# Output projection in blocks of 126 features, the last group of heads taken straight from SBUF, and half of the second projection's blocks summed earlier

## Chip, cores and metric

One core of a Trainium2 chip runs the whole program. The metric is the device time of one execution in microseconds. The core has a matrix engine (PE, its weight loads shown as PEld), a vector engine (DVE), an activation engine (ACT), a general engine (POOL), and SyncE (SP), which here only issues DMAs. Each engine takes its instructions in the order in which the program lists them and waits for the others through semaphores.

## The reference

Two independent parts are computed and set side by side in the output's columns (2048 rows, 576 + 576 columns):

```python
# A: sliding-window attention, 32 heads of 18 features, window 256, over x (2048 x 576)
q, k, v = x @ wqkv                       # per head
p = softmax(where(0 <= i - j < 256, q k^T / sqrt(18), -1e9))
a = concat_heads(p @ v) @ wo             # wo: 576 x 576
# B: a state-space convolution over u (2048 x 576)
K = real(sum_n C[d,n] dB[d,n] exp(dt A[d,n] l))
b = causal_conv(u, K) + u * Dskip
out = concatenate([a, b], axis=-1)
```

## The kernel before

A first part (up to about 550 us) projects q, k and v, builds the convolution's taps, and writes the intermediate results to DRAM. The second part, `attention`, is one hand-written instruction order for all engines: no scheduler moves anything.

**Units and items.** Attention works in 16 units: 2 halves of 1024 queries by 8 groups of 4 heads (unit i has half i // 8, group i % 8). A unit has 6 items (2 chunks of 512 queries by 3 banks of score blocks), so there are 96 items; the loop runs n from 0 to 97. In step n, `merge` interleaves several generators by their share of work done: the scores and exponentials of item n (`scores`, PE then ACT, then POOL's triangular masks), row maxima of a later unit (`gmax`, PE then DVE), the weighted values of item n - 2 (`values`, PE), 2 or 3 steps of the convolution (`conv`), and, from n = 64, one step of the output projection of the first half in every second n (`wo(0)`).

**Convolution.** `conv` has 16 rounds of transforms on PE, ACT, DVE and POOL, then 16 rounds that read its result back (tiles ho and tx from h), load u on POOL's queue (tiles X and t), multiply it by Dskip on POOL, and add on DVE. The second kind of round runs in about the last 20 steps.

**Quotients.** `values` accumulates 4 heads in one PSUM tile of 128 rows: each head has 32 rows, 18 of values, and its row 18 is the softmax denominator. After a chunk's last bank ACT copies it to `osb` (line 704). After a unit's last item `norm` is appended to a list and advanced one yield per step n: four small DMAs bring the denominators into 128x32 (`den`, line 714); a reciprocal (line 717); a spread to 128x1024 (line 720); a matmul with a block matrix `same` copies it to all rows of a head (line 726); DVE multiplies (727); ACT makes the fp16 high part (728) and DVE the low part (730); POOL's queue stores 18 rows of each head to the DRAM tensor `od`, high and low parts (734). After the loop the list is run to its end.

**Output projection.** `od` has 576 features by 2048 positions, twice. `wo_load` splits wo into `woh` and `wol` with 5 blocks of rows: four of 128 features and a last one in which 64 features stand twice, for the high and the low part. `wo_operands(c)` loads 512 positions of `od` in four DMAs on SP (lines 846 to 849). `wo(hf)` has 16 steps for two chunks c, each for 128 positions by 288 output columns: 14 matmuls (5 high x high, 5 high x low, 4 low x high; line 173), a scaled copy by ACT from PSUM (line 862), and after two steps a DMA of 128 output rows (`ya`, two buffers; `after(1, ...)` issues it one item later). `wo(0)` is spread over the items; `wo(1)` runs alone after everything else.

All small PSUM results (gmax, conv, norm, wo) take turns in one pool `ring` of three banks, so a matmul group waits until the group three before it has been evacuated.

## Time and profile before

| | us |
|---|---|
| runs shown: median (lowest, highest) | 1151.99 (1150.27, 1154.17) |
| the profiled execution, its own time | 1151.56 |
| its span, first to last instruction | 1149.8 |
| PE busy | 912.0 (79%) |
| DVE busy | 704.7 (61%) |
| ACT busy | 624.3 (54%) |
| POOL busy | 527.1 (46%) |

All times of rows are microseconds from the span's start unless marked ns. A row of the timeline gives start, duration, engine, line, operation, tiles (out<-in), shape and count; in square brackets stands how long the engine was idle before it and what ended that. A row of the chain gives start, duration, engine and line. A row of the busy time by stretch gives, for each engine, the busy time and the number of instructions, then the granted PE clock (1.00 is full), the mean busy share of the 16 DMA engines and GB/s. A row of the groups gives line, engine, operation, count, busy time and mean ns, then idle time before the group. Matmuls are pipelined, so the busy time of one is longer than its share of a stream of them.

### The profile page before, as it was taken

How to read it: one execution, taken by the hardware profiler on the slowest of the kernel's cores; microseconds unless marked ns; L12 is line 12 of the kernel's file. 1: busy time of each engine (PE TensorE's matmuls, PEld its weight loads, DVE VectorE, ACT ScalarE, POOL GpSimd, SP SyncE). 2: the span in 40 equal slices, each digit the busy share in tenths (PEclk: the TensorE clock that was granted, in tenths of full speed). 3: DMA queues.
4: the chain of work that ended last, by engine and by line, in shares of the span. 5: the costliest groups of instructions: out<-in, count | busy, mean ns of one | idle time of the engine just before them, and what ended most of it. 6: DMA issues, size and time to landing. Idle time of an engine off the chain costs nothing.

```text
span 1149.8 us, 26992 instructions
## 1 busy us (share of the span) xinstructions
PE 912.0 (79%) x10380; PEld 446.9 (39%) x10380; DVE 704.7 (61%) x1789; ACT 624.3 (54%) x955; POOL 527.1 (46%) x626
## 2 busy tenths in 40 slices
PE   1535979897978889866888889888889899896648
PEld 0313546455545655423333333333333333332216
DVE  2879656866776552366666778777776665653220
ACT  1785778767878742331455555555655554544312
POOL 0014324543545330102356656667666655679810
PEclk9757889898989889997799999999999999988859
DMA  9564423433342325984334554644336453558742
GB/s 271 150 190 137 101 46 89 109 92 86 84 109 59 78 61 128 228 247 131 98 120 125 140 151 138 169 132 136 110 107 166 134 160 110 166 153 227 202 123 84
DMA packets 157682, 153.59 MB, mean 134 GB/s; under 512 B 37777, under 2 KB 136017, under 8 KB 157361
## 3 DMA queue, kind: packets, MB, share of 16 engines
q1 hardware_dynamic: 149600, 132.68, 42.6%
q0 software_dynamic: 6448, 15.19, 5.0%
q10 hardware_dynamic: 1504, 3.99, 1.3%
q8 instruction: 82, 1.34, 0.5%
q14 instruction: 48, 0.39, 0.1%
HBM read 89.79 MB, written 61.60 MB: 132 GB/s over the span
## 4 chain that ended last, share of the span: by engine, by line
PE 46%; DVE 17%; DMA 13%; ACT 9%; issue 7%; POOL 6%; SPq 2%; DVEq 0%; ACTq 0%; POOLq 0%
PE pp L173 8%; PE po L696 6%; PE r L637 5%; PE r L501 5%; PE r L173 4%; PE r L508 3%; PE r L726 3%; PE ST L673 3%; PE kp L419 3%; PE pp L462 3%; DMA K<-in_wqkv_dram 2%; PE x L315 2%; DMA gk<-g 2%; POOL P L684 2%; DVE qb L629 1%
## 5 line engine op out<-in xcount | busy, mean ns | idle before, releaser
L640 DVE CUSTOM_DVE_ANT_0 jk<-r,bias 128x288 f32<-128x288 f32 (+7 forms) x512 | 206.6, 435 | 113.4 <-PE r L637 110.7
L675 ACT ACTIVATE P<-ST,esc 128x1024 f32<-128x1024 f32 (+1 forms) x192 | 203.3, 1060 | 95.5 <-PE ST L673 89.7
L381 POOL TENSOR_TENSOR m<-A,tr 128x1024 f32<-128x1024 f32 x72 | 149.3, 2094 | 195.4 <-PE kp L419 139.0
L684 POOL TENSOR_SCALAR_AFFINE_SELECT P<-P 128x512 f32<-128x512 f32 x240 | 158.2, 690 | 99.5 <-ACT P L675 97.3
L637 PE MATMUL r<-K,qb 128*64 128x288 f16 (+7 forms) x1024 | 134.3, 300 | 27.0 <-DVE t L528 6.2
L696 PE MATMUL po<-P,V 128*32 128x256 f32 (+2 forms) x1408 | 116.9, 404 | 4.7 <-ACT osb L704 2.2
L536 POOL TENSOR_TENSOR Y<-t,t 64x288 f32<-64x288 f32 x64 | 54.5, 852 | 140.0 <-DVE t L531 86.6
L637 PEld LDWEIGHTS <-qb 128*64 128x64 f16 x1024 | 60.3, 111 | 129.7 <-issue 75.9
L419 PE MATMUL kp<-Q,m 128*32 128x64 f32 x4608 | 87.4, 228 | 26.4 <-DVE Q L402 10.8
L419 PEld LDWEIGHTS kp<-Q,m 128*32 128x32 f32 x4608 | 74.4, 115 | 55.0 <-issue 42.9
L462 PE MATMUL pp<-ut,w 128*128 128x288 f32 x128 | 51.9, 530 | 43.3 <-DMA ut<-in_u_dram 22.9
L673 PE MATMUL ST<-Q,K 64*128 64x384 f16 (+2 forms) x704 | 75.3, 284 | 2.4 <-DMA Q<-m 2.4
L728 ACT ACTIVATE oh<-osb 128x512 f16<-128x512 f32 x32 | 20.2, 630 | 103.8 <-DVE osb L727 103.8
L238 DVE SCALAR_TENSOR_TENSOR qst<-pp,qst 128x512 f16<-128x512 f32 x36 | 24.7, 686 | 65.3 <-ACT qst L237 65.2
L726 PE MATMUL r<-spread,heads 128*128 128x512 f32 x64 | 40.1, 715 | 27.1 <-DVE spread L720 18.9
L129 ACT ACTIVATE g<-pp 128x288 f32<-128x288 f32 (+1 forms) x84 | 34.3, 447 | 39.7 <-DMA gk<-g 21.1
L501 PE MATMUL r<-tx,w 128*64 128x288 f32 x256 | 46.9, 447 | 11.0 <-DMA tx<-gx 9.5
L537 POOL TENSOR_TENSOR Y<-t,t 64x288 f32<-64x288 f32 x64 | 53.4, 835 | 3.8
L462 PEld LDWEIGHTS pp<-ut,w 128*128 128x128 f32 x128 | 28.6, 242 | 63.5 <-issue 19.0
L327 ACT ACTIVATE ab<-k 128x512 f32<-128x512 f32 (+1 forms) x54 | 31.9, 590 | 38.3 <-DVE k L326 37.9
L508 PE MATMUL r<-Y,i 128*128 128x288 f32 x128 | 49.1, 466 | 3.5 <-DVE m L640 1.5
L173 PE MATMUL pp<-xh,wl 128*128 128x512 f16 x180 | 49.0, 396 | 0.0
(159 smaller groups left out, 1743.7 us busy)
## 6 DMA issues: line engine op xcount, KB each, us to landing
gx<-g SPq DMA_DIRECT2D x32, 288.0 KB
qd<-qst SPq DMA_DIRECT2D x72, 128.0 KB
gk<-g SPq DMA_DIRECT2D x16, 576.0 KB
tx<-gx SPq DMA_DIRECT2D x16, 576.0 KB
tk<-gk SPq DMA_DIRECT2D x16, 576.0 KB
h<-ho SPq DMA_DIRECT2D x16, 576.0 KB
raw<-in_xT_dram SPq DMA_DIRECT2D x16, 512.0 KB
Q<-qd SPq DMA_DIRECT2D x32, 216.0 KB
```

The source lines that it names most:

```text
L173: self.nc.tensor.matmul(ps, u, v, start=(i == 0), stop=(i == len(ops) - 1))
L381: self.nc.gpsimd.tensor_tensor(m, A[:, ch, a0:a0 + 8].unsqueeze(3).to_broadcast(sh), tr[:, ch, part, 0:8].unsqueeze(2).to_broadcast(sh), o ...
L419: nc.tensor.matmul(kp[32 * st:32 * st + 32, c % 2 * JJ2 + j, :], m[:, ch, a0:a0 + 32], Q[:, ch, term % 2, :], start=(term == 0), stop=(ter ...
L462: nc.tensor.matmul(ps, self.w1[:, part, :], src[:, o:o + k], start=True, stop=True)
L501: nc.tensor.matmul(ps[64 * par:64 * par + 64], w2[:, par, 64 * part:64 * part + 64], t[:, 2 * hs:2 * hs + 2, par, :], start=True, stop=True)
L508: nc.tensor.matmul(ps, i1[:, par, :], Y[par], start=True, stop=True)
L637: nc.tensor.matmul(ps[64 * b:64 * b + 64, :n], self.qb[:, b, t, :], d["K"][:, b, k0:k0 + n], start=True, stop=True, skip_group_check=True)
L640: nc.vector.tensor_tensor_reduce(out=jk[:, :n], in0=ps[:, :n], in1=self.bias[:, 288 - n:], scale=1.0, scalar=-3e38, op0=OP.add, op1=OP.max ...
L673: nc.tensor.matmul(ps[:, u, o:o + n], d["K"][h, jp, k0:k0 + 128], d["Q"][h, jp, q0:q0 + n], start=True, stop=True, skip_group_check=True)
L675: nc.scalar.activation(pt[:, 2 * jp:2 * jp + 2, lo:hi], ps[:, :, lo:hi], AF.Exp, scale=self.esc)
L684: nc.gpsimd.affine_select(v, v, pattern=[[0, 4], [sg, 128]], compare_op=OP.is_ge, fill=0.0, base=-1 if far else 0, channel_multiplier=-sg)
L696: nc.tensor.matmul(self.po[32 * j:32 * j + 32, t0 * 128:t1 * 128], V[:, kb * 76 + 19 * j:kb * 76 + 19 * j + 32], pt[:, j, o:o + (t1 - t0) ...
```

## The change

- wo's rows are laid out on the host as four blocks of 126 features (7 heads of 18) and a fifth block with the last group of 4 heads (72 features) at rows 0 to 17 of each 32, the layout that a normalised unit has in SBUF. `wo_load` loads each column slice with one DMA.
- Units 7 and 15, the last group of each half, are no longer stored to `od`: their quotients stay in a tile `h7` and feed the fifth block directly. A step of the projection has 12 matmuls on four blocks and 3 on `h7`.
- Unit 15 gets its own normalisation, `norm_last`, for each chunk of 512: a matmul with a new block matrix `sums` puts each head's denominator on all its rows, DVE takes the reciprocal of 128x512, multiplies, and the two parts go to `h7`. The first chunk is begun at n = 95, the second after the loop.
- The first half's projection (`wo_first`) runs spread over n = 62 to 85.
- For the second half, blocks 0 and 1 are loaded at n = 84 and 88 and summed in n = 87 to 96 (`wo_part`, 16 steps of 6 matmuls); ACT copies the scaled sums to tiles that the convolution no longer uses. After the loop `wo_operands` loads blocks 2 and 3, and `wo_rest` has 16 steps of 9 matmuls; DVE adds the stored sum at evacuation.

The diff:

```diff
@@ -72,12 +72,15 @@
         bias[p, 1, p % 32 + 1:] = -1e30
     c["c_w1"], c["c_w2"], c["c_i1"], c["c_i2"] = w1, w2, i1, i2
     c["c_id"], c["c_bias"] = np.eye(128), bias
-    c["c_heads"] = np.concatenate([np.kron(np.eye(4), np.ones((32, 32))), np.tile(np.eye(32), (4, 1))], axis=1)
+    row = np.zeros((32, 32))
+    row[18] = 1.0
+    c["c_heads"] = np.concatenate([np.kron(np.eye(4), np.ones((32, 32))), np.tile(np.eye(32), (4, 1)),
+                                   np.kron(np.eye(4), row)], axis=1)
     return {k: np.ascontiguousarray(v.astype(ml_dtypes.bfloat16 if k in mult else np.float32)) for k, v in c.items()}
 
 
 def merge(*streams):
-    live = [[g, n, 0] for g, n in streams]
+    live = [[g, n, 0] for g, n in streams if n]
     while live:
         s = min(live, key=lambda t: t[2] / t[1])
         try:
@@ -598,9 +601,9 @@
                 nc.vector.memset(d["K"][h + 32:h + 64], -32768.0)
             self.sets.append(d)
         self.od = self.p["dram"].tile([2, D, L], F16, name="od")
-        hd = ap.tile([128, 160], F32, name="heads")
+        hd = ap.tile([128, 288], F32, name="heads")
         nc.sync.dma_start(hd, a["c_heads"])
-        self.same, self.pick = hd[:, 0:128], hd[:, 128:160]
+        self.same, self.pick, self.sums = hd[:, 0:128], hd[:, 128:160], hd[:, 160:288]
 
     def cols(self, hf):
         q0 = HQ * hf
@@ -703,6 +706,21 @@
                 self.osb[i] = self.p["o"].tile([128, HQ], F32, name="osb")
             nc.scalar.activation(self.osb[i][:, c * 512:c * 512 + 512], self.po, AF.Copy)
 
+    def norm_last(self, c):
+
+        nc, osb, cs = self.nc, self.osb[15], slice(c * 512, c * 512 + 512)
+        ps = self.p["ring"].tile([128, 512], F32, name="r")
+        nc.tensor.matmul(ps, self.sums, osb[:, cs], start=True, stop=True)
+        rb = self.p["n1"].tile([128, 512], F32, name="rb")
+        nc.vector.reciprocal(rb, ps)
+        yield
+        h = self.h7[1]
+        nc.vector.tensor_tensor(osb[:, cs], osb[:, cs], rb, op=OP.mult)
+        nc.scalar.activation(h[:, 0, cs], osb[:, cs], AF.Copy)
+        yield
+        nc.vector.tensor_tensor(h[:, 1, cs], osb[:, cs], h[:, 0, cs], op=OP.subtract)
+        yield
+
     def norm(self, i):
 
 
@@ -719,7 +737,10 @@
         sh = [128, 32, 32]
         nc.vector.tensor_tensor(X, den.unsqueeze(1).to_broadcast(sh), self.pick.unsqueeze(2).to_broadcast(sh), op=OP.mult)
         yield
-        h = np_.tile([128, 2, HQ], F16, name="oh16")
+        if i == 7:
+            h = self.h7[0] = self.p["h7"].tile([128, 2, HQ], F16, name="h7")
+        else:
+            h = np_.tile([128, 2, HQ], F16, name="oh16")
         for c in range(2):
             cs = slice(c * 512, c * 512 + 512)
             ps = self.p["ring"].tile([128, 512], F32, name="r")
@@ -729,7 +750,7 @@
             yield
             nc.vector.tensor_tensor(h[:, 1, cs], osb[:, cs], h[:, 0, cs], op=OP.subtract)
         yield
-        for j in range(4):
+        for j in range(4 if i != 7 else 0):
             f0 = 72 * g + 18 * j
             nc.gpsimd.dma_start(self.od[:, f0:f0 + 18, HQ * hf:HQ * hf + HQ].rearrange("a p n -> p a n"),
                                 h[32 * j:32 * j + 18])
@@ -743,7 +764,7 @@
         merge((self.gmax(0), 35), (part(conv, 12), 12))
         self.begin(1)
         items = [(i, c, b) for i in range(16) for c in range(2) for b in range(3)]
-        wo0, wl = self.wo(0), self.wo_load()
+        wo0, wo1, wl, self.acc, self.h7 = self.wo_first(), self.wo_part(), self.wo_load(), [], {}
         for n in range(len(items) + 2):
             self.begin(n)
             streams = []
@@ -776,28 +797,41 @@
                 streams.append((part(conv, k), k))
             if 20 <= n < 52 and n % 2 == 0:
                 next(wl, 0)
-            if n in (60, 72):
-                self.wo_operands((n - 60) // 12)
-            if n >= 64 and n % 2 == 0:
-                streams.append((part(wo0, 1), 1))
+            if n in (59, 67):
+                self.wo_operands((n - 59) // 8, 0, 4)
+            if 62 <= n < 86:
+                k = share(n - 62, 16, 24)
+                streams.append((part(wo0, k), k))
+            if n == 86:
+                for _ in wo0:
+                    pass
+            if n in (84, 88):
+                self.wo_operands(2 + (n - 84) // 4, 0, 2)
+            if 87 <= n < 97:
+                k = share(n - 87, 16, 10)
+                streams.append((part(wo1, k), k))
+            if n == 95:
+                self.h7[1] = self.p["h7"].tile([128, 2, HQ], F16, name="h7")
+                norms.append(self.norm_last(0))
             merge(*streams)
             norms = [g for g in norms if next(g, 0) is None]
-            if n >= 2 and (n - 2) % 6 == 5:
+            if n >= 2 and (n - 2) % 6 == 5 and n < 97:
                 norms.append(self.norm(items[n - 2][0]))
                 next(norms[-1])
-        for g in norms:
-            for _ in g:
-                pass
+        norms.append(self.norm_last(1))
+        while norms:
+            norms = [g for g in norms if next(g, 0) is None]
         for n in range(3):
             self.begin(len(items) + 2 + n)
             for _ in conv:
                 pass
-        for _ in wo0:
+        for _ in wo1:
             pass
-        self.wo_operands(2)
-        self.wo_operands(3)
-        for _ in self.wo(1):
-            pass
+        for c in (2, 3):
+            self.wo_operands(c, 2, 4)
+        for c in (2, 3):
+            for _ in self.wo_rest(c):
+                pass
 
     def wo_load(self):
         nc, a, wp = self.nc, self.a, self.p["wo"]
@@ -808,7 +842,7 @@
 
         def raw(c):
             t = wp.tile([128, 5, 144], F32, name="raw%d" % (c % 2))
-            self.load_rows(t, a["wo"], slice(c % 4 * 144, c % 4 * 144 + 144))
+            nc.sync.dma_start(t, a["wo"][:, :, c % 4 * 144:c % 4 * 144 + 144])
             return t
 
         nx = raw(0)
@@ -838,34 +872,63 @@
                 nc.vector.scalar_tensor_tensor(self.osc, self.pz, 2.0 ** -13, po, op0=OP.mult, op1=OP.mult)
                 yield
 
-    def wo_operands(self, c):
-
-        nc, wp, cs = self.nc, self.p["wo2"], slice(c * 512, c * 512 + 512)
-        oh = wp.tile([128, 5, 512], F16, name="oh")
-        ol = wp.tile([128, 4, 512], F16, name="ol")
-        nc.sync.dma_start(oh[:, 0:4], self.od[0, 0:512, cs].rearrange("(k p) n -> p k n", p=128))
-        nc.sync.dma_start(oh[0:64, 4], self.od[0, 512:576, cs])
-        nc.sync.dma_start(oh[64:128, 4], self.od[1, 512:576, cs])
-        nc.sync.dma_start(ol, self.od[1, 0:512, cs].rearrange("(k p) n -> p k n", p=128))
-        self.ops[c] = oh, ol
-
-    def wo(self, hf):
-        nc, a, wp = self.nc, self.a, self.p["wo2"]
-        for c in range(2 * hf, 2 * hf + 2):
-            oh, ol = self.ops[c]
+    def wo_operands(self, c, k0, k1):
+
+        nc, cs = self.nc, slice(c * 512, c * 512 + 512)
+        if c not in self.ops:
+            self.ops[c] = [self.p["wo2"].tile([126, 4, 512], F16, name=n) for n in ("oh", "ol")]
+        for e, t in enumerate(self.ops[c]):
+            nc.sync.dma_start(t[:, k0:k1], self.od[e, 126 * k0:126 * k1, cs].rearrange("(k p) n -> p k n", p=126))
+
+    def wo_mm(self, c, t, h, k0, k1, last):
+
+        ps = self.p["ring"].tile([128, 512], F32, name="r")[:, :288]
+        (oh, ol), ts, ws = self.ops[c], slice(t * 128, t * 128 + 128), slice(h * 288, h * 288 + 288)
+        ops = [(o[:, k, ts], w[0:126, k, ws]) for k in range(k0, k1)
+               for o, w in ((oh, self.woh), (oh, self.wol), (ol, self.woh))]
+        if last:
+            x, o = self.h7[c // 2], c % 2 * 512 + t * 128
+            ops += [(x[:, e, o:o + 128], w[:, 4, ws]) for e, w in ((0, self.woh), (0, self.wol), (1, self.woh))]
+        for i, (l, r) in enumerate(ops):
+            self.nc.tensor.matmul(ps, l, r, start=(i == 0), stop=(i == len(ops) - 1))
+        return ps
+
+    def wo_first(self):
+
+        for c in range(2):
             for t in range(4):
-                y = wp.tile([128, D], F32, name="ya")
+                y = self.p["wo2"].tile([128, D], F32, name="ya")
                 for h in range(2):
-                    ps = self.p["ring"].tile([128, 512], F32, name="r")
-                    self.mm14(ps[:, :288], (self.woh, self.wol), (oh, ol), slice(h * 288, h * 288 + 288),
-                              slice(t * 128, t * 128 + 128), flip=True)
-                    nc.scalar.activation(y[:, h * 288:h * 288 + 288], ps[:, :288], AF.Copy, scale=self.osc)
+                    ps = self.wo_mm(c, t, h, 0, 4, True)
+                    self.nc.scalar.activation(y[:, h * 288:h * 288 + 288], ps, AF.Copy, scale=self.osc)
                     yield
                 r = c * 512 + t * 128
-                if hf:
-                    nc.sync.dma_start(a["out"][r:r + 128, 0:D], y)
-                else:
-                    self.after(1, nc.sync.dma_start, a["out"][r:r + 128, 0:D], y)
+                self.after(1, self.nc.sync.dma_start, self.a["out"][r:r + 128, 0:D], y)
+
+    def wo_part(self):
+
+        p, acc = self.p, self.acc
+        for i in range(2):
+            t = p["fs"].tile([128, 4, 288], F32, name="tk")
+            acc += [t[:, k] for k in range(4)]
+            t = p["wo"].tile([128, 2, 288], F32, name="raw%d" % i)
+            acc += [t[:, k] for k in range(2)]
+            acc += [p["fy"].tile([128, 288], F32, name="Y%d" % k) for k in range(2)]
+        for n in range(16):
+            ps = self.wo_mm(2 + n // 8, n // 2 % 4, n % 2, 0, 2, False)
+            self.nc.scalar.activation(acc[n], ps, AF.Copy, scale=self.osc)
+            yield
+
+    def wo_rest(self, c):
+        for t in range(4):
+            y = self.p["wo2"].tile([128, D], F32, name="ya")
+            for h in range(2):
+                ps = self.wo_mm(c, t, h, 2, 4, True)
+                self.nc.vector.scalar_tensor_tensor(y[:, h * 288:h * 288 + 288], ps, self.osc,
+                                                    self.acc[(c - 2) * 8 + t * 2 + h], op0=OP.mult, op1=OP.add)
+                yield
+            r = c * 512 + t * 128
+            self.nc.sync.dma_start(self.a["out"][r:r + 128, 0:D], y)
 
     def build(self):
         nc, a = self.nc, self.a
@@ -906,7 +969,7 @@
                 self.dsk = self.p["fc"].tile([128, D], F32, name="dsk")
                 nc.sync.dma_start(self.dsk, a["dsk"].partition_broadcast(128))
                 for n, b, s in (("fs", 2, None), ("fy", 2, None), ("att", 1, None), ("m", 2, None), ("P", 4, None),
-                                ("v", 4, None), ("o", 3, None), ("n", 2, None), ("n1", 1, None), ("wo", 1, None), ("wo2", 2, None),
+                                ("v", 4, None), ("o", 3, None), ("n", 2, None), ("n1", 1, None), ("h7", 1, None), ("wo", 1, None), ("wo2", 2, None),
                                 ("stp", 2, PSUM), ("ops", 1, PSUM), ("ring", 3, PSUM)):
                     self.pool(e1, n, b, s)
                 self.att_setup()
@@ -922,12 +985,15 @@
     arrays = {
         "xT": np.ascontiguousarray(inputs["A_x"][0].T),
         "wqkv": np.ascontiguousarray(inputs["A_wqkv"][:, np.r_[np.arange(1152).reshape(64, 18).T.ravel(), 1152:1728]]),
-        "wo": np.ascontiguousarray(inputs["A_wo"]),
+        "wo": np.zeros((128, 5, D), np.float32),
         "u": np.ascontiguousarray(inputs["B_u"][0]),
         "ldt": np.ascontiguousarray(inputs["B_log_dt"][perm][None]),
         "ldtn": np.ascontiguousarray(np.tile(inputs["B_log_dt"][perm].reshape(NQ, GC).T, (3, 1))),
         "dsk": np.ascontiguousarray(inputs["B_Dskip"][None]),
     }
+    arrays["wo"][0:126, 0:4] = inputs["A_wo"][0:504].reshape(4, 126, D).transpose(1, 0, 2)
+    for j in range(4):
+        arrays["wo"][32 * j:32 * j + 18, 4] = inputs["A_wo"][504 + 18 * j:522 + 18 * j]
     for n in S4_PARAMS:
         arrays["p_" + n] = np.ascontiguousarray(inputs["B_" + n].T[:, perm])
     for n in ("A_re", "A_im"):
```

## The prediction

> **What bounds the kernel now.** I read the busy shares first, then the busy time by stretch, then the chain of work that ended last.
>
> ```profile
> PE 912.0 (79%) x10380; PEld 446.9 (39%) x10380; DVE 704.7 (61%) x1789; ACT 624.3 (54%) x955; POOL 527.1 (46%) x626
> ```
>
> ```profile
> core 0: us, PE busy (x) PEld busy (x) DVE busy (x) ACT busy (x) POOL busy (x), PEclk, DMA share, GB/s
> 889.30:985.00 95.70, 87.94 (x774) 36.96 (x773) 59.46 (x216) 53.18 (x75) 53.23 (x80) 1.00 0.44 122
> 985.00:1036.00 51.00, 45.42 (x408) 19.06 (x411) 29.07 (x99) 23.39 (x27) 40.07 (x65) 0.93 0.64 182
> 1036.00:1096.00 60.00, 41.55 (x338) 14.47 (x338) 19.75 (x34) 22.14 (x26) 50.20 (x73) 0.86 0.76 208
> 1096.00:1114.80 18.80, 3.75 (x4) 1.18 (x4) 4.32 (x7) 1.26 (x2) 4.77 (x8) 0.54 0.31 82
> 1114.80:1149.80 35.00, 30.62 (x224) 22.88 (x224) 0.00 (x0) 8.02 (x16) 0.00 (x0) 0.89 0.34 117
> ```
>
> Four regimes follow one another. From the first output-projection step (889) to 1036 PE is 89 to 92% busy and sets the pace. From 1036 to 1096 POOL is (50.2 of 60 us), PE has 18 us idle. From 1096 to 1114.8 all engines mostly wait: the last unit's normalisation goes through DRAM. From 1114.8 only PE works, on 16 steps of 14 matmuls (x224). The chain shows that tail step by step:
>
> ```profile
> 1095.39 0.61 ACT osb L704
> ...
> 1097.84 2.24 DMA den<-osb
> ...
> 1108.36 1.76 POOL od L734 x3
> 1110.12 2.26 DMA od<-oh
> ...
> 1113.57 4.43 DMA ol<-od
> 1118.05 28.05 PE r L173 x214
> 1146.12 0.50 ACT ya L862
> ```
>
> From the last attention block's copy (1095.4) to the end (1149.8) are 54.4 us; call 1095.4 T. The change shortens what lies behind T and pays with work ahead of T.
>
> **The tail.** Three things leave it: the den round trip, the store of unit 15 with the loads that wait for it, and 5 of 14 matmuls in each of 16 steps (9 are left: 6 on blocks 2 and 3, 3 on the quotients). Two paths now lead to the first matmul.
>
> The first is unit 14's store and its loads, which stay. Their prices:
>
> ```profile
> 1095.39 0.68 DVE L730 TENSOR_TENSOR oh<-osb,oh 128x512 f16<-128x512 f32 x1
> 1096.37 2.42 POOL L734 DMA_DIRECT2D od<-oh  x4 [5.99 <-DVE oh L730]
> 1110.88 0.39 SPq L846 DMA_DIRECT2D oh<-od  x1
> 1112.40 0.49 SPq L847 DMA_DIRECT2D oh<-od  x1
> 1114.82 1.38 PE L173 MATMUL r<-woh,oh 128*128 128x288 f16 x5 [9.14 <-DMA oh<-od]
> ```
>
> Unit 14's four store issues begin 1.0 us behind T. Unit 15's began at 1108.36 and had landed when the load that needed the last of them issued, at 1112.40: 4.0 us. So the loads of blocks 2 and 3 issue at T+5.0. The load issued at 1110.88 carried 512 KB and let PE start 3.9 us later; the new ones carry 252 KB each, so I take 3.2 (bounds 2.5 and 3.9). PE starts at T+8.2. On SP these loads stand behind the last output rows of the convolution, whose issues ended at 1100.5, T+5.1: no further wait. A rule speaks against this piece: the Trainium skill, "DMA: Bandwidth & Descriptors", section "Why a DMA increments its semaphore by 16 and not by 1", has a DMA use the largest number of engines up to 16 that divides the outer dimension, so 126 rows would go over 14 engines and 128 over 16. By it my estimate is half a microsecond more, 1144.1 in place of the forecast below; no run before shows a 126-row transfer.
>
> The second path is the new normalisation of unit 15's second half: copy (0.6), one fp32 matmul, reciprocal of 128x512, multiply, ACT copy, subtraction. No reciprocal of that width exists in the trace; there are these:
>
> ```profile
> L717 DVE RECIPROCAL den<-den x16: 341/348/353, 602.8 to 1100.2; 128x32 f32<-128x32 f32 x16
> L155 DVE RECIPROCAL or<-op x1: 165/165/165, 713.4 to 713.4; 128x1 f32<-128x1 f32 x1
> 1089.58 0.69 DVE L727 TENSOR_TENSOR osb<-osb,r 128x512 f32<-128x512 f32 x1 [1.49 <-PE r L726]
> ```
>
> The line through 165 ns for 1 column and 348 for 32 gives 5.9 ns a column, so 165 + 511 x 5.9 = 3.2 us. Bounds: 0.7 us, if it ran like the multiply of the same width, and 5.6, if all 348 ns scaled with 32 columns. I take 3.2, since two points carry it. The path is then 0.6 + 2.0 (a pair of passes at low clock) + 3.2 + 0.7 + 0.6 + 0.7 = T+7.8, level with the loads; at 5.6 it is T+10.2. Even that blocks only the evacuation by DVE, not PE: with three PSUM buffers PE can run three steps ahead, which at low clock last 6.5 us. The Trainium skill, "VectorE: DVE Perf Modes", section "First, the fixed hardware budget", says that the reciprocal repeats its divide 8 times; at the page's 0.96 GHz that makes 512 x 8 / 0.96 = 4.3 us, an estimate. By it the sum is 1 us worse, for the other reciprocal below.
>
> ```profile
> 1118.98 1.41 PE L173 MATMUL r<-woh,oh 128*128 128x288 f16 x5
> 1120.18 1.17 PE L173 MATMUL r<-wol,oh 128*128 128x288 f16 x4
> ...
> 1142.49 0.78 PE L173 MATMUL r<-woh,oh 128*128 128x288 f16 x5
> ...
> 1144.21 0.78 PE L173 MATMUL r<-woh,oh 128*128 128x288 f16 x5
> ```
>
> A step of 14 takes 1.72 us late in the tail (0.123 a matmul); early, five starts take 1.20 (0.24 each, half clock). The 224 matmuls ran from 1114.8 to 1146.1, 31.3 us, which is 224 x 0.123 = 27.6 and 3.7 of low clock and waiting. I keep 3.5 of that: 144 x 0.123 + 3.5 = 21.2 us. Evacuation moves to DVE as a multiply-add with the stored sum. The rows for its cost:
>
> ```profile
> L404 DVE SCALAR_TENSOR_TENSOR Q<-sn,mg 128x512 f32<-128x512 f32 x36 | 24.4, 679 | 0.0
> L862 ACT ACTIVATE ya<-r,osc 128x288 f32<-128x288 f32 x32 | 16.0, 502 | 58.6 <-PE r L173 46.7 <-DMA oh<-od 11.9
> ```
>
> Between 0.4 (679 ns by 288 columns of 512) and 0.7, hidden under the 1.1 us of a step except for the last. The last evacuation ended at 1146.6 and the span at 1149.8; the 3.2 us stay. New tail: 8.2 + 21.2 + 0.5 + 3.2 = 33.1, against 54.4: **21.3 less**.
>
> **Ahead of T: the first half's projection.** It runs in items 62 to 86 in place of every second item from 64 to 94, and its steps have 15 matmuls, not 14. Up to item 86, 16 x 15 = 240 matmuls replace 12 x 14 = 168: 72 more, 5.1 old steps, while PE sets the pace. What one such step costs in the pace of the units, and its own time:
>
> ```profile
> 761.45 0.59 ACT L704 ACTIVATE osb<-po 128x512 f32<-128x512 f32 x1
> ...
> 824.18 0.59 ACT L704 ACTIVATE osb<-po 128x512 f32<-128x512 f32 x1
> ...
> 891.01 0.59 ACT L704 ACTIVATE osb<-po 128x512 f32<-128x512 f32 x1
> ...
> 984.55 0.59 ACT L704 ACTIVATE osb<-po 128x512 f32<-128x512 f32 x1
> 949.02 1.82 PE r L173 x14
> ```
>
> These copies come every three items. There are 4, 4 and 5 of those gaps between the four rows: 5.23, 5.57 and 6.24 us an item. Only the last stretch has projection steps, one in two items. So a step cost 2 x 0.67 = 1.3 us, against the units of the same half, or 2 x 1.01 = 2.0, against the earlier ones; PE's own time is 1.82. I take 1.6: 5.1 x 1.6 = **8.2 more**, bounds 6.6 and 10.2. Loads issued on SP at items 59 and 67 move by a few items, before anything needs them; unit 7's store leaves POOL, which is not the bound there; the loads of wo become one DMA of 360 KB in place of three with the same sum, and the chain passes through one of them:
>
> ```profile
> 649.60 7.92 DMA raw<-in_wo_dram
> ```
>
> Since the bytes stay, only two issues each are saved. All these I cost at nothing; the last may gain a microsecond or two.
>
> **Ahead of T: the partial sums.** In items 87 to 96 there are 16 x 6 = 96 matmuls where 4 old steps (56) stood: 40 more, 4.9 us of PE, and 16 ACT copies of 0.5 us for 4. The cover is PE's idle time:
>
> ```profile
> 1040.00:1050.00 10.00, 2.33 (x6) 0.72 (x6) 3.35 (x5) 0.32 (x1) 9.61 (x14) 0.65 1.01 281
> 1050.00:1070.00 20.00, 19.57 (x171) 7.40 (x174) 6.97 (x11) 11.12 (x13) 17.99 (x28) 0.92 0.76 197
> 1080.00:1088.00 8.00, 1.23 (x9) 0.73 (x6) 3.06 (x5) 0.40 (x1) 6.26 (x9) 0.74 0.56 165
> ```
>
> Two stretches leave PE idle 14 us, but PE takes its queue in order and idles behind a blocked matmul, and between them it is full. Bounds 0 (all in the holes) and 5.5 (all paid). I take **3**. The four loads of 252 KB that come on SP in items 84 and 88 meet DMA engines that are saturated at 1040 (share 1.01); the four output stores of 288 KB that used to fall here go earlier, so this pair I cost at nothing, or 2 us if it delays one load of u.
>
> **Ahead of T: the wide reciprocal of item 95.** It sits in DVE's queue in front of two output additions of the convolution, and holds one of three PSUM buffers:
>
> ```profile
> 1088.49 1.06 PE L726 MATMUL r<-spread,heads 128*128 128x512 f32 x1
> 1091.79 0.71 PE L574 MATMUL r<-tx,i 128*64 128x288 f32 x4
> ```
>
> The sum matmul would end 1.1 us behind 1089.55, and the reciprocal at 1093.8; PE's next but one matmul group, at 1091.79, needs its buffer and starts **2 us later**. Bounds 0 and 4.4.
>
> **Sum.** -21.3 + 8.2 + 3 + 2 = -8.1 us. The profiled execution took 1151.56 us, span 1149.8; so 1143.5. The median of the runs shown is 1151.99, 0.4 above; from there 1143.9, and I give 1143.6.
>
> **Rivals.** *The added work is hidden.* PE's idle time takes the sums, the early steps cost 1.3, the reciprocal is short: -21.3 + 6.6 + 0 + 0 = -14.7, 1137. For it: 18 us idle in 1036 to 1096. Against: PE's order.
>
> *Everything is paid.* All bounds at their dear end: -21.3 + 10.2 + 5.5 + 4.4 = -1.2, 1150.6, no change. For it: PE full in 1050 to 1070.
>
> *Slower: the partial sums run on the chain at half clock.* With waiting matmuls in front of them, 96 x 0.24 = 23 us replace 4 x 1.82 = 7.3: 15.7 more; with 8.2 and 2 that is 25.9 against 21.3, +4.6, 1156.4. It decides once the work ahead of T grows by over 21.3. For it: clock 0.65 and 0.74 in the two holes. Against: the clock is 0.92 between them, and more PE work fills the holes.
>
> *The projection in the tail does not shrink in time,* since output stores or DVE set its pace: -21.3 + 9.8 back (80 matmuls) leaves 1153. Against: the stores kept up with 3.43 us a tile, and 2.2 would be asked.
>
> **Chances.** Forecast 0.60 (own range 1139 to 1149), hidden 0.13, all paid 0.09, half clock 0.14, tail not shrunk 0.04. Less than 0.3% either way (3.5 us) is what a measurement of this kernel cannot tell from no change. The forecast's dear edge lends a little to no change: faster 0.70, same 0.13, slower 0.17. The range, 1136 to 1155, leaves out most of the half-clock case and a margin at the low end.
>
> **What would show it.** Right: from the last osb copy to the end 33 us, the den issue of unit 15 gone, first tail matmul 8 us behind that copy, and that copy near 1108. Wrong: a wide reciprocal far from 3.2 us; items 62 to 80 at 6.2 us as before (the extra steps were free) or over 7; a wait of DVE on out_dram<-ya in the tail; partial sums of twice 0.74 us with PE last in the chain at 1036 to 1096.

## The result, and the profile after

The changed kernel takes 1141.16 us (median of 4 runs, 1136.85 to 1142.89) beside 1153.08 for the kernel before in the same session: 0.9887 of it, interval 0.9843 to 0.9932. Two more sessions gave 0.9925 [0.9898, 0.9951] and 0.9936 [0.9915, 0.9956], that is 11.9, 10.6 and 8.1 us less. The forecast was 1143.6, or 8.1 less.

The totals of one kernel scatter by up to ±6 us (1134 to 1146 for the changed kernel), and much of that lies in the first part, which no experiment's edit touches: the first osb copy came at 569 to 579 us in fourteen profiles. So I compare by stretches that the 32 osb copies (numbered from 0; 31 is T) mark. Means of two profiles of before and three of after:

| stretch | before | after | difference |
|---|---|---|---|
| start to copy 0 | 573.1 | 572.9 | -0.2 |
| copies 0 to 19 | 300.3 | 300.8 | +0.5 |
| copies 19 to 28 (steps n = 62 to 88) | 163.7 | 168.6 | +4.9 |
| copies 28 to 31 (n = 89 to 97) | 59.6 | 64.9 | +5.3 |
| T to the span's end | 54.4 | 32.2 | -22.2 |

A copy marks the values of an item, which run two steps after its scores: copy 19 stands at the end of step n = 61 and copy 28 in step 88. An item number below is the step n, by the scores that run in it. So the third stretch holds 13 projection steps before (182 matmuls), and 16 steps and 3 partial sums after (258); the fourth holds 3 projection steps before (42) and 13 partial sums after (78).

Busy shares, and busy time by stretch, of the profiled execution of the changed kernel (1142.89 us, span 1141.2); its columns are those shown for before:

```profile
PE 921.1 (81%) x10412; PEld 450.9 (40%) x10412; DVE 717.9 (63%) x1805; ACT 624.2 (55%) x955; POOL 519.8 (46%) x618
```

```profile
core 0: us, PE busy (x) PEld busy (x) DVE busy (x) ACT busy (x) POOL busy (x), PEclk, DMA share, GB/s
889.00:985.00 96.00, 89.01 (x777) 39.31 (x774) 56.20 (x201) 50.55 (x71) 48.84 (x75) 0.98 0.41 121
985.00:1045.30 60.30, 55.62 (x513) 24.41 (x510) 33.49 (x121) 31.88 (x40) 46.63 (x74) 1.00 0.67 178
1045.30:1110.00 64.70, 49.58 (x368) 18.04 (x368) 21.79 (x34) 25.74 (x36) 48.78 (x71) 0.84 0.70 187
1110.00:1117.90 7.90, 1.13 (x2) 0.30 (x2) 5.99 (x6) 1.22 (x3) 2.41 (x4) 0.77 0.51 134
1117.90:1141.20 23.30, 19.46 (x144) 14.38 (x144) 8.29 (x16) 0.00 (x0) 0.00 (x0) 0.93 0.34 126
```

The last line is the new tail: 144 matmuls instead of 224, evacuated by 16 DVE instructions. The third line is new too: in 64.7 us no engine is full, neither PE (49.6) nor POOL (48.8).

The chain of waits near the end, start and duration:

```profile
1085.11 4.61 DMA out_dram<-t
1089.73 4.76 DMA tx<-h
1094.51 2.62 DMA out_dram<-t
...
1110.93 1.82 POOL od L755 x3
1112.76 2.37 DMA od<-oh
1115.14 0.33 SPq L881
1115.48 0.06 issue
1115.53 3.09 DMA ol<-od
1118.63 0.05 issue
1118.67 18.81 PE r L893 x142
1137.51 0.52 DVE ya L927
```

The den round trip and unit 15's store are gone; unit 14's store and its loads lead to the tail. Ahead of T the chain goes through output stores and readbacks on SP's queue.

The timeline around T:

```profile
1110.02 0.58 ACT L707 ACTIVATE osb<-po 128x512 f32<-128x512 f32 x1
1110.65 1.13 PE L713 MATMUL r<-osb,heads 128*128 128x512 f32 x2 [0.75 <-ACT osb L707]
1110.93 2.41 POOL L755 DMA_DIRECT2D od<-oh  x4 [9.29 <-DVE oh L751]
1111.81 3.36 DVE L715 RECIPROCAL rb<-r 128x512 f32<-128x512 f32 x1 [0.57 <-PE r L713]
1115.14 0.33 SPq L881 DMA_DIRECT2D oh<-od  x1
1116.66 0.69 DVE L721 TENSOR_TENSOR h<-osb,h 128x512 f16<-128x512 f32 x1 [0.70 <-ACT h L719]
1117.91 0.42 PE L893 MATMUL r<-woh,oh 126*128 126x288 f16 x1 [6.14 <-DMA oh<-od]
...
1121.05 0.32 PE L893 MATMUL r<-woh,oh 126*128 126x288 f16 x1
```

PE starts at T + 7.9, waiting for the loads and not for the quotients (the last of them is done at T + 7.3), and leaves half clock 3 us later: the matmuls start 0.24 us apart up to 1121.05 and 0.12 apart from there.

### The profile page after: what moved, and what is told of

Its sections match the earlier page's. It is cut to its first block, busy times and chain, and to the rows that moved or that the text cites. A ratio compares the mean times of both kernels' runs of the same rounds, so it can differ in the third digit from the quotient of the medians.

```text
span 1141.2 us, 27005 instructions
## 1 busy us (share of the span) xinstructions
PE 921.1 (81%) x10412; PEld 450.9 (40%) x10412; DVE 717.9 (63%) x1805; ACT 624.2 (55%) x955; POOL 519.8 (46%) x618
## 4 chain that ended last, share of the span: by engine, by line
PE 50%; DVE 19%; DMA 10%; ACT 9%; issue 7%; SPq 4%; POOL 1%; DVEq 0%; ACTq 0%; POOLq 0%
PE pp L176 8%; PE po L699 7%; PE r L504 6%; PE r L640 6%; PE r L893 4%; PE r L511 4%; PE ST L676 3%; PE pp L465 3%; PE kp L422 3%; PE r L747 3%; PE x L318 2%; DMA gk<-g 2%; DVE tr L362 2%; DMA K<-in_wqkv_dram 2%; DVE jk L643 1%
## 5 line engine op out<-in xcount | busy, mean ns | idle before, releaser
L687 POOL TENSOR_SCALAR_AFFINE_SELECT P<-P 128x512 f32<-128x512 f32 x240 | 158.1, 688 | 107.2 <-ACT P L678 105.0
L539 POOL TENSOR_TENSOR Y<-t,t 64x288 f32<-64x288 f32 x64 | 54.4, 849 | 149.8 <-DVE t L534 147.9
L422 PE MATMUL kp<-Q,m 128*32 128x64 f32 x4608 | 87.9, 230 | 27.7 <-DVE Q L405 10.6
L241 DVE SCALAR_TENSOR_TENSOR qst<-pp,qst 128x512 f16<-128x512 f32 x36 | 24.7, 686 | 64.2 <-ACT qst L240 64.1
L749 ACT ACTIVATE oh<-osb 128x512 f16<-128x512 f32 x28 | 17.6, 630 | 78.9 <-DVE osb L748 78.9
L132 ACT ACTIVATE g<-pp 128x288 f32<-128x288 f32 (+1 forms) x84 | 34.5, 447 | 39.7 <-DMA gk<-g 19.9
L330 ACT ACTIVATE ab<-k 128x512 f32<-128x512 f32 (+1 forms) x54 | 31.9, 591 | 36.5 <-DVE k L329 36.0
L176 PE MATMUL pp<-xh,wh 128*128 128x512 f16 x180 | 47.8, 387 | 1.2 <-DVE xh L233 1.2
L504 PE MATMUL r<-tk,w 128*64 128x288 f32 x256 | 46.4, 443 | 2.8 <-DVE m L643 1.0
```

Of the source, the lines that this page charges most:

```text
L176: self.nc.tensor.matmul(ps, u, v, start=(i == 0), stop=(i == len(ops) - 1))
L422: nc.tensor.matmul(kp[32 * st:32 * st + 32, c % 2 * JJ2 + j, :], m[:, ch, a0:a0 + 32], Q[:, ch, term % 2, :], start=(term == 0), stop=(ter ...
L504: nc.tensor.matmul(ps[64 * par:64 * par + 64], w2[:, par, 64 * part:64 * part + 64], t[:, 2 * hs:2 * hs + 2, par, :], start=True, stop=True)
L687: nc.gpsimd.affine_select(v, v, pattern=[[0, 4], [sg, 128]], compare_op=OP.is_ge, fill=0.0, base=-1 if far else 0, channel_multiplier=-sg)
```

## Experiments

Theory 1 was the prediction's own sum: the tail gives 21 to 22 us, and PE, in its own order, pays for most of what is put ahead of T. The rival was that one of the pieces costs nothing or brings nothing. Stretches are from one profile of each kernel; times are medians of all runs, and "before" is the kernel before on the same chip.

| run | us (runs) | before | ratio, interval | 19 to 28 | 28 to 31 | tail |
|---|---|---|---|---|---|---|
| a_same | 1141.38 (6) | 1152.02 | 0.9925 [0.9898, 0.9951] | 166.7 | 65.2 | 32.4 |
| b_no_sums | 1136.40 (5) | 1152.02 | 0.9871 [0.9848, 0.9893] | 167.7 | 60.8 | 32.6 |
| c_no_first | 1116.07 (6) | 1152.02 | 0.9710 [0.9682, 0.9738] | 144.7 | 65.5 | 32.9 |
| d_sums_in_tail | 1147.08 (12) | 1152.02 | 0.9973 [0.9950, 0.9997] | 165.7 | 64.3 | 43.9 |
| e_recip_late | 1138.67 (6) | 1150.69 | 0.9901 [0.9869, 0.9932] | 169.6 | 63.8 | 31.9 |
| f_den | 1140.40 (6) | 1150.69 | 0.9897 [0.9868, 0.9927] | 169.6 | 63.8 | 33.2 |
| g_warm | 1139.27 (6) | 1150.69 | 0.9900 [0.9867, 0.9934] | 169.6 | 62.7 | 31.7 |
| h_direct_only | 1140.30 (6) | 1150.69 | 0.9903 [0.9873, 0.9933] | 162.3 | 63.7 | 43.3 |
| before_again | 1153.75 (1) | | | 163.1 | 60.7 | 54.3 |
| a_again | 1142.01 (11) | 1150.10 | 0.9936 [0.9915, 0.9956] | 169.6 | 64.7 | 32.9 |
| i_late | 1132.22 (6) | 1150.10 | 0.9841 [0.9804, 0.9878] | 158.1 | 59.2 | 38.1 |
| k_no_stores | 1133.99 (6) | 1150.10 | 0.9871 [0.9838, 0.9903] | 168.1 | 56.6 | 32.1 |

**a_same.** The changed kernel, no edit.

> The changed kernel again, beside the three that follow. Theory 1 (the tail gives back about 22 us, and the work moved ahead of the last copy costs about 12): 1141 us, 11 to 13 below the kernel before. Theory 2 (the work moved ahead is hidden, and the measured difference is mostly scatter between executions): the stretch from the last osb copy to the end 31 us as in the first profile, but the copy itself earlier by several us in a second profile.

1141.38: the reference for b, c and d.

**b_no_sums.** What do the partial sums cost where they stand?

```diff
 def wo_part(self):
-            ps = self.wo_mm(2 + n // 8, n // 2 % 4, n % 2, 0, 2, False)
-            self.nc.scalar.activation(acc[n], ps, AF.Copy, scale=self.osc)
+            self.nc.scalar.activation(acc[n], self.dsk[:, n % 2 * 288:n % 2 * 288 + 288], AF.Copy, scale=self.osc)
```

> The 96 matmuls of the partial sums in items 87 to 96 are left out; ACT's 16 copies stay and read another tile, the loads stay. Own time of the matmuls: 96 x 0.123 = 11.8 us. Theory 1 (three fifths of PE's time is paid there, 3 of the 4.9 us that were added): 7 us less than the changed kernel, 1134. Rival (PE's idle time hides them): no change, 1141. Rival (PE sets the pace there now): 12 less, 1129.

5.0 us less than a_same, where theory 1 said 7; 4.1 of it lies between copies 28 and 31 (60.8 beside 64.9). The 96 matmuls are 11.8 us of PE at 0.123 each, so some 40% is paid: neither hidden nor paid in full.

**c_no_first.** What does the first half's projection cost in items 62 to 86?

```diff
-            if n in (59, 67):
-                self.wo_operands((n - 59) // 8, 0, 4)
-            if 62 <= n < 86:
-                k = share(n - 62, 16, 24)
-                streams.append((part(wo0, k), k))
-            if n == 86:
-                for _ in wo0:
-                    pass
```

> The first half's projection is left out with its loads, copies and stores: 240 matmuls, 29.5 us of PE's own time in items 62 to 86. Theory 1 (1.6 us paid for each 1.82 us of PE, 88%): 26 us less than the changed kernel, 1115. Rival (half of it is hidden): 1126. Rival (more than its own time is paid, 2.0 for 1.82): 1109.

25.3 us less in all, and 23.9 between copies 19 and 28 (144.7 beside 168.6): 80% of the 29.5 us of 240 matmuls, or 1.49 us for each of 16 steps, with their loads, copies and stores, which c leaves out too. The 13 steps of before in this stretch, set against the same 144.7, come to 1.46 each, or to 1.6 if the 3 partial sums that c holds there cost the 2 us that b shows between copies 27 and 28 (12.2 beside 14.2). So the mean price is 1.5 to 1.6, and the prediction's 1.6 stands. But the difference of the two kernels, 4.9 us for 76 more matmuls, is only 1.0 for 15 of them. The lengths of single items (from the start of one item's first exponential on ACT to that of the next) show how:

| item | 63 | 64 | 65 | 66 | 67 | 68 | 69 | ... | 82 | 83 | 84 |
|---|---|---|---|---|---|---|---|---|---|---|---|
| c_no_first | 4.41 | 4.05 | 10.12 | 5.60 | 3.23 | 6.38 | 4.67 | | 3.13 | 10.04 | 6.77 |
| h_direct_only (even items) | 4.22 | 6.12 | 8.65 | 7.49 | 3.23 | 7.78 | 4.35 | | 5.07 | 7.80 | 7.92 |
| after (two items of three) | 5.56 | 6.11 | 10.13 | 7.50 | 5.01 | 6.42 | 6.12 | | 5.07 | 7.29 | 7.92 |
| i_late (odd items) | 5.56 | 4.05 | 9.79 | 5.61 | 5.01 | 6.42 | 6.12 | | 3.13 | 9.14 | 5.86 |

A step costs 1.9 to 2.1 us in items 64, 66 and 82, 1.2 in item 63, and nothing in items 65 and 83, which take 10 us in c. The price of a step is that of its item, and a later item can give some back: item 83 has no step in the changed kernel and takes 7.29, not 10.04, so that its steps in 81, 82 and 84 cost 1.4 us together over items 81 to 84 (24.7 beside 23.3).

**d_sums_in_tail.** The first half stays early, the sums go back behind T (15 matmuls a step there).

```diff
-            if 87 <= n < 97:
-                k = share(n - 87, 16, 10)
-                streams.append((part(wo1, k), k))
 def wo_rest
-                ps = self.wo_mm(c, t, h, 2, 4, True)
-                self.nc.vector.scalar_tensor_tensor(...)
+                ps = self.wo_mm(c, t, h, 0, 4, True)
+                self.nc.scalar.activation(y[:, h * 288:h * 288 + 288], ps, AF.Copy, scale=self.osc)
```

> The partial sums are undone: 15 matmuls in each of the tail's 16 steps, evacuated by ACT; blocks 0 and 1 are still loaded early. Theory 1: tail 11.8 us longer, middle 7 shorter, 1146. Rival (the sums are free in the middle): 1153. Rival (the sums cost there what they save in the tail): 1141.

5.7 us more than a_same. Busy time by stretch in its tail:

```profile
1117.00:1152.10 35.10, 31.25 (x232) 23.72 (x232) 0.00 (x0) 8.02 (x16) 0.00 (x0) 0.92 0.21 79
```

The tail grows by 11.7 (43.9 beside 32.2) and, by the medians, 6.0 come back ahead of T: near b's price, measured the other way. The stretches of the profiled execution (1153.78, the slowest of its 12) give back only 3.5 (2.9 and 0.6).

**e_recip_late, f_den, g_warm.** Three small terms: the wide reciprocal of item 95 begun after the loop; unit 15's denominators brought by the old den path, still without its store and now without both wide reciprocals; 18 unread matmuls of 128x512 between T and the tail.

```diff
 e_recip_late
-                norms.append(self.norm_last(0))
...
-        norms.append(self.norm_last(1))
+        norms.append(self.norm_last(0))
...
+        for _ in self.norm_last(1):
+            pass
 f_den
+        elif i == 15:
+            h = self.h7[1]
...
-        for j in range(4 if i != 7 else 0):
+        for j in range(4 if i % 8 != 7 else 0):
 g_warm
+        ps = self.p["ring"].tile([128, 512], F32, name="r")
+        for i in range(18):
+            self.nc.tensor.matmul(ps, self.woh[:, 0, 0:128], self.woh[:, 1, 0:512], start=True, stop=True)
```

> The normalisation of unit 15's first chunk, with its 3.36 us reciprocal, is begun after the loop, not at item 95. Theory 1 (the reciprocal holds up DVE and a PSUM buffer by 2 us ahead of the last copy, and the tail has room for it): 2 us less than the changed kernel, 1139. Rival (POOL and the DMAs set the pace there, the reciprocal is hidden): 1141, or 1 to 2 more where DVE then delays the tail's evacuation.

> Unit 15's denominators go the old way (four small DMAs, 128x32 reciprocal, spread, matmul), the quotients still stay in SBUF. Theory 1 (the tail waits for unit 14's store and loads, to 7.9 us behind the last copy; the old way delivers the first quotients at 10.7 and frees DVE at 12.7; no wide reciprocal at item 95): 1 to 2 us more in the tail, 2 less ahead, 1141. Rival (the denominators' round trip was what the tail waited for): 4 more, 1145.

> 18 matmuls of 128x512 that nobody reads are added on PE between the last copy and the first matmul of the tail, while PE would wait 6 us for the loads. Theory 1 (the first 13 matmuls of the tail take 0.24 us for lack of activity, 0.123 later): 1.5 to 2 us less, 1139.5. Rival (the added matmuls end after the loads have landed and push the tail): up to 2 more, 1143.

Beside the changed kernel's own 0.9887, 0.9925 and 0.9936 in three sessions (up to 5.6 us apart), the three ratios (0.9897 to 0.9901) say nothing, so nothing under some 5 us is read from these totals. By stretches: e takes 1.1 off copies 28 to 31 (63.8), and g, whose edit lies behind T, takes 2.2 there. But they do so in different places (table of gaps below). g's 2.2 lie between copies 28 and 29, which scatter; e's lie between 30 and 31, where the first reciprocal stands: 20.2 and 20.1 in e and f, which have none there, beside 21.1 to 22.1 in the six kernels and repeats that hold it and the sums. So that reciprocal costs about 1 us, and not 2. f's tail is 33.2 beside 32.2 (31.2 to 32.9 in three profiles): the den round trip beside the loads costs about 1 us. So the long wait behind T goes as soon as nothing has to be stored and loaded after den; den itself may stay. g brings PE to full clock before the tail:

```profile
1104.78:1114.00 9.22, 5.93 (x26) 2.56 (x27) 5.97 (x6) 1.21 (x3) 2.41 (x4) 1.00 0.55 151
```

but its tail is 31.7, within the scatter of 31.2 to 32.9, where 1.5 to 2 less were expected. The half clock comes all the same, only later:

```profile
1112.76 0.30 PE L896 MATMUL r<-woh,oh 126*128 126x288 f16 x1 [2.34 <-DMA oh<-od]
...
1114.53 0.45 PE L896 MATMUL r<-wol,oh 126*128 126x288 f16 x1
...
1117.88 0.29 PE L896 MATMUL r<-woh,h 128*128 128x288 f16 x1
```

From 1114.4 to 1117.7 the matmuls start 0.24 us apart again, 3.3 us at half clock beside 3.1 in the changed kernel. The unread matmuls moved that stretch and did not remove it.

**h_direct_only.** Blocks of 126 and direct quotients alone: no sums (the tail's steps are those of d), and the first half's steps back at every second item up to 94.

```diff
-            if n in (59, 67):
-                self.wo_operands((n - 59) // 8, 0, 4)
-            if 62 <= n < 86:
...
-            if n in (84, 88):
-                self.wo_operands(2 + (n - 84) // 4, 0, 2)
-            if 87 <= n < 97:
...
+            if n in (60, 72):
+                self.wo_operands((n - 60) // 12, 0, 4)
+            if n >= 64 and n % 2 == 0:
+                streams.append((part(wo0, 1), 1))
+            if n in (84, 97):
+                self.wo_operands(2 + (n - 84) // 13, 0, 2)
```

> Only the blocks of 126 and the direct quotients are kept: the first half's projection is paced as before (items 64 to 94), and the second half's 16 steps have 15 matmuls in the tail; blocks 0 and 1 are loaded at items 84 and 97. Theory 1 (by the prediction's prices: tail 9.5 below before, 16 matmuls more in the middle, 2 for the reciprocal): 6 below before, 1147. Rival (the round trip through DRAM is not what is saved, all of the gain is in the fewer tail matmuls): as before, 1153. Rival (the early projection and the sums bring nothing over it): 1141.

Theory 1 fell here: 1140.30, not 1147. Its ratio of 0.9903 is that of e, f and g (0.9897 to 0.9901), which hold the early first half and the sums and ran beside it on the same chip. The tail is 43.3, so direct quotients alone save 11.1 of the 22.2; the sums save the other 11. What they and the earlier first half add ahead of T takes as much back by the totals, and 7.5 of it by the stretches from copy 19 on of h's one profile. So half of this change brings between nothing and 4 us as it is placed.

**before_again, a_again, i_late, k_no_stores.** Why are copies 28 to 31 longer, and can the half that brings nothing be placed better? k leaves out the convolution's output stores, 64 of 72 KB; i spreads the first half over items 62 to 92 (odd items, one step in two), puts half of the sums and the first wide reciprocal behind the loop, and moves the second pair of loads from item 88 to 95.

```diff
 k_no_stores
-            for k in range(4):
-                self.after(1, nc.sync.dma_start, outv[4 * qd + k], y[32 * k:32 * k + 32])
 i_late
-            if 62 <= n < 86:
-                k = share(n - 62, 16, 24)
+            if 62 <= n < 93:
+                k = share(n - 62, 16, 31)
...
-            if n in (84, 88):
-                self.wo_operands(2 + (n - 84) // 4, 0, 2)
-            if 87 <= n < 97:
-                k = share(n - 87, 16, 10)
-                streams.append((part(wo1, k), k))
+            if n in (84, 95):
+                self.wo_operands(2 + (n - 84) // 11, 0, 2)
+            if 88 <= n < 96:
+                streams.append((part(wo1, 1), 1))
...
-                norms.append(self.norm_last(0))
-        norms.append(self.norm_last(1))
+        norms.append(self.norm_last(0))
...
+        for _ in self.norm_last(1):
+            pass
...
+        for _ in wo1:
+            pass
```

> The kernel before once more, for a second sample of its stretches. In the one profile so far the copies of osb number 28 to 31 (the last ten items) lie 58.4 us apart, against 62.7 to 65.5 in nine executions of changed kernels, also in those that have no partial sums. Theory 1 (the change itself adds some 6 us there, by its loads, output rows and reciprocal beside the convolution's transfers): 58 to 59 us again, from the 19th to the 28th copy 164, tail 54.4. Theory 2 (this stretch scatters by itself and the first profile was a lucky one; the change adds nothing there): 62 to 65 us again, with the same total of about 1151.

> The changed kernel as it is, on the same chip as the two below. Both theories: 1141, some 10.5 below the kernel before; from the 28th to the 31st copy of osb 64 to 65 us; tail 31 to 32.5.

> The changed kernel without the convolution's last step: its output rows (64 stores of 32 rows) are not written, so those columns of the output stay unset; the additions that make the rows stay. Theory 1 (in the last ten items the chain goes through SP's queue and the DMAs, since the output stores stand on it in front of the readbacks tx and the loads of the projection): from the 28th to the 31st copy of osb 52 to 56 us in place of 64.7, total 1130 to 1133. Theory 2 (POOL with 49 of 65 us busy, and PE, which takes the sums in order, set the pace; stores are beside it): 62 to 65 us, total 1139 to 1142.

> An attempt at a better version: the first half's projection is paced over items 62 to 92 in place of 62 to 85, the partial sums of the first 512 positions fall in items 88 to 95, those of the second 512 behind the loop, where PE waits some 7 us for the last loads (8 steps of 6 matmuls, 48 x 0.123 = 5.9 us at full clock, up to 11.8 at half), their loads are issued at item 95, and the normalisation of the last unit's first chunk is begun behind the loop. Theory 1 (PE's own order pays for what is put ahead of the last copy; leaving the sums out gave 5 us, half of them are moved into idle time): 1136 to 1137, of it 2 to 3 from items 87 to 97, 2 from items 62 to 86, with up to 1.6 given back in the tail. Theory 2 (transfers on SP's queue set the pace of the last ten items, so fewer matmuls there bring nothing, and the pace of items 62 to 92 only moves cost from one stretch to the next): 1140 to 1142, tail up to 6 us longer where the sums run at half clock.

before_again has 60.7 between copies 28 and 31, midway between the theories: some of the first sample's 58.4 was luck, but the change does add there, 4.0 to 6.8 us by the five profiles. Gap by gap, in us between neighbouring copies:

| run | 27 to 28 | 28 to 29 | 29 to 30 | 30 to 31 |
|---|---|---|---|---|
| before, before_again | 15.6, 15.6 | 24.2, 26.8 | 14.0, 14.0 | 20.2, 19.9 |
| after, a_again, a_same | 14.2, 14.2, 14.2 | 29.9, 30.0, 29.5 | 13.7, 13.7, 13.7 | 21.1, 21.1, 22.1 |
| b_no_sums | 12.2 | 26.5 | 10.9 | 23.3 |
| d_sums_in_tail | 11.8 | 29.5 | 11.6 | 23.2 |
| c_no_first | 14.7 | 30.7 | 13.7 | 21.2 |
| e_recip_late | 14.2 | 29.9 | 13.7 | 20.2 |
| f_den | 14.2 | 30.0 | 13.7 | 20.1 |
| g_warm | 14.2 | 27.8 | 13.7 | 21.2 |
| h_direct_only | 15.8 | 26.0 | 14.3 | 23.5 |
| i_late | 14.7 | 25.9 | 14.7 | 18.7 |
| k_no_stores | 14.2 | 20.2 | 15.2 | 21.1 |

Of the 5.3 us that the change adds, 4.3 lie between copies 28 and 29. The sums are not what adds them: d has none there and takes 29.5.

k takes 8.3 off copies 28 to 31 and 8.0 off the total: SP's queue and its transfers set the pace there, as theory 1 had it. The kernel before has the same stores, and it was not run without them, so k does not show that they are what the change made dearer. The DMA issues on SP in the changed kernel's trace (start, duration, line, out<-in, count):

```profile
1034.90 1.89 SPq L123 DMA_DIRECT2D out_dram<-t  x4
1036.90 1.79 SPq L555 DMA_DIRECT2D ho<-h  x4
1038.79 1.80 SPq L123 DMA_DIRECT2D out_dram<-t  x4
1040.69 3.43 SPq L123 DMA_DIRECT2D Q<-m  x4
1044.16 0.58 SPq L881 DMA_DIRECT2D oh<-od  x1
1044.78 0.43 SPq L881 DMA_DIRECT2D ol<-od  x1
1045.31 1.78 SPq L555 DMA_DIRECT2D tx<-h  x4
1047.18 1.91 SPq L555 DMA_DIRECT2D ho<-h  x4
```

SP issues almost back to back, mostly 0.4 to 0.6 us a DMA, and stores and readbacks take turns. The chain of waits, first of the changed kernel and then of k at the same place:

```profile
1045.72 0.42 SPq L555
1046.19 6.34 DMA tx<-h
1052.90 3.90 DMA out_dram<-t
1056.93 0.46 DVE t L579
1057.68 2.91 DVE spread L738
```

```profile
1049.62 1.96 POOL t L559 x4
1051.60 1.42 POOL X L573
1053.01 1.44 POOL X L559 x3
1054.44 7.38 DMA X<-in_u_dram
```

Without the stores SP drops out of the chain and POOL's loads of u take over. Whether SP's issuing or the stores' share of the DMA engines counts more was not separated. The readback that takes 6.34 us follows directly on the pair of loads at 1044.16; in i, where that pair is moved, the same readback takes

```profile
1033.81 4.03 DMA tx<-h
```

and the gap between copies 28 and 29 is 25.9 us beside 29.9. h, which moves the pair to item 97, has 26.0, and before, without it, 24.2 and 26.8; seven of the nine profiles that hold both the pair and the stores have 29.5 to 30.7 in that gap. That the pair is the cause is still only argued: b (26.5) and g (27.8) keep it and have short gaps, and no kernel that moves it alone was run.

i beats both kernels: 9.8 us less than a_again, with intervals that do not meet. By stretches, -10.5 (158.1 for 168.6), -5.7 (59.2 for 64.9) and +5.9 in the tail (38.1 for 32.2), a sum of -10.3. I had expected only 2 us of it from items 62 to 86. Three steps fewer in that stretch are 4.5 at 1.5, and two partial sums fewer some 1 more; the rest fits the table of items, since two of i's steps fall in items 65 and 83, and the others in the cheaper odd ones. A kernel that differs in this alone was not run. In the tail I had expected to give back 1.6 at most. Its 5.9 have this shape on PE:

```profile
1095.70 0.29 PE L893 MATMUL r<-woh,ol 126*128 126x288 f16 x1
1097.84 0.28 PE L893 MATMUL r<-woh,oh 126*128 126x288 f16 x1 [1.85 <-DVE rb L715]
...
1103.22 0.40 PE L893 MATMUL r<-woh,oh 126*128 126x288 f16 x1 [4.48 <-DVE rb L715]
```

The two wide reciprocals, now both behind T, hold two of the three PSUM banks, and the sums wait 1.85 and 4.48 us for them. Taking the first of them back to item 95 should free part of that; it was not run.

## Why the prediction was right, point by point

The total and the sign were right, and so was the main mechanism: a tail some 22 us shorter, part of it paid back ahead of T. Ahead of T one price missed its bounds, and another sum came right by luck. The terms, in the prediction's order:

- **Tail, -21.3: measured -22.2.** Loads issue at T + 5.1 (forecast 5.0) and PE starts at T + 7.9 (8.2). 144 matmuls take 19.6 us, and 20.8 and 21.5 in a_same and a_again (21.2): of 3.5 us of low clock and waiting 1.9 to 3.8 came. Evacuation on DVE is 518 ns, within the forecast 0.4 to 0.7, and the end is 3.2 as said.
- **The 252 KB load**, 3.2 us from issue to PE: measured 2.7 to 2.8. By the rule of the Trainium skill, "DMA: Bandwidth & Descriptors", section "Why a DMA increments its semaphore by 16 and not by 1", my estimate was half a microsecond more for 126 rows. No run here shows whether it holds: the load came sooner than the sum had it, but no load of 128 rows and equal size was run beside it.
- **First half's projection, +8.2, bounds 6.6 and 10.2: +4.9, below its bounds.** The step that failed is "5.1 x 1.6". The mean price was right (1.5 to 1.6), but the added steps do not fall in mean items: the marginal price was 1.0. The price also came from a reading that is a little off: 7 of the 15 items between 891.01 and 984.55 have a step, not one in two, so its two prices are 1.4 and 2.2, not 1.3 and 2.0; this makes the forecast no better. Items 63 to 80 took 6.3 to 6.4 us each beside 6.0 to 6.2 before, neither free nor over 7.
- **Partial sums, +3, bounds 0 and 5.5, and reciprocal, +2: +5.3 together.** The sum is right by luck in its parts. The sums cost 5 to 6 us by the totals of b and d (5.0 and 3.5 by their stretches), of which 4.1 and 0.6 show between copies 28 and 31; the reciprocal cost about 1, not 2. The three projection steps that leave these copies, 42 matmuls, should have given 4.5 back at c's price, yet the stretch grew. Of its growth 4.3 lie between copies 28 and 29, behind the pair of loads on SP's queue that I had "cost at nothing, or 2 us if it delays one load of u". If the pair is the cause, it delayed a readback on SP; that is not shown. And three output stores of 288 KB fell there before (issued at 1042.8, 1068.9 and 1090.6), not the four that I counted.
- **The wide reciprocal, 3.2 us**, from a line through two points:

```profile
L715 DVE RECIPROCAL rb<-r x2: 3358/3358/3358, 1102.3 to 1111.8; 128x512 f32<-128x512 f32 x2
```

  3.36 us: the line through the 1 and 32 column rows holds to 512 columns within 5%. The estimate from the Trainium skill, "VectorE: DVE Perf Modes", section "First, the fixed hardware budget", was 4.3; the measurement decides.
- **"Half clock" and "the tail does not shrink"** are both out: the clock is 0.84 between copies 28 and 31, and the work ahead of T grew by 10.5 us, not over 21; from PE's start in the tail DVE is busy 8.3 of 23.3 us.
- **What would show it.** The tail of 33 (31.2, 32.4 and 32.9 in three profiles) and the start 8 us behind the copy came. The copy near 1108 came in two of three profiles (1110.0, 1100.1 and 1111.7); its place also holds the scatter of the first part. The prediction said nothing of the finding that matters most: that direct quotients alone would bring as much, within 4 us.

## What to carry to other kernels

Price a moved step in the place where it lands, item by item and with what a later wait gives back, and not by the mean of its stretch: the same 1.85 us of PE cost between nothing and 2 us here. Work taken out of a tail is only won if the place that takes it has room on every queue; moving 11 us of sums out of the tail and the first half out of their way netted 4 us at most. With steps, sums and loads placed anew (i) the whole gained some 10 us more. Where no engine is full, look at the queue that issues the DMAs.

## What the runs showed that I had not expected

- The reciprocal on DVE takes 165, 348 and 3358 ns for 1, 32 and 512 fp32 columns: about 6.3 ns a column from 32 on.
- Matmuls on 126 rows run at the pace of 128 rows, 0.123 us for 288 columns; a step of 9 takes 1.1 us.
- PE's clock fell to half 1.6 us into the tail of g although it had been full at its start: 4 us of matmuls, then 2.3 us of waiting, preceded it.
- Attention repeats to 0.1 us in most gaps between osb copies (20.0, 18.3 to 18.4 and 20.9 to 21.0 us in nine executions with the first half's steps placed alike), while the first 570 us scatter by 10.
